# A GFNet and MLP layer on one core: the first stage done one tile at a time

## The chip, the core and the metric

The kernel runs on one NeuronCore of a Trainium2 chip. Five engines work side by side, each through its own instructions in order: TensorE (PE in the profile, with its weight loads shown as PEld), VectorE (DVE), ScalarE (ACT), GpSimd (POOL) and SyncE (SP), which here only issues transfers between HBM and the on-chip memory SBUF. The engines wait for each other on semaphores. The metric is the device time of one execution, in microseconds; lower is better.

## The reference

One batch of S = 2048 rows with D = 576 channels goes through a spectral filter and then an MLP with 4608 hidden channels, each behind a layer norm, each with a residual. Everything is fp32.

```python
def _layernorm(x, axis=-1, eps=1e-5):
    m = jnp.mean(x, axis=axis, keepdims=True)
    v = jnp.var(x, axis=axis, keepdims=True)
    return (x - m) / jnp.sqrt(v + eps)
...
        X = jnp.fft.rfft2(x, axes=(-2, -1))      # x: layer norm of A_x
        X = X * (w_r + 1j * w_i)
        y = jnp.fft.irfft2(X, s=(S, D), axes=(-2, -1))
...
        h = jnp.einsum("bsd,df->bsf", x, w1)     # x: layer norm of h
        h = jnp.maximum(h, zero)
        return jnp.einsum("bsf,fd->bsd", h, w2)
...
    h = x + _A_ref(_layernorm(x, axis=-1), A_w_r, A_w_i)
    h2 = h + _B_ref(_layernorm(h, axis=-1), B_w1, B_w2)
```

## The kernel before

The transforms are matrix products with constant cosine and sine tables. The program has four stages, one behind the other on TensorE.

The first stage takes the 16 tiles of x (128 rows by 576 channels each; rows 16 apart lie in one tile) through the layer norm and the first step of the transform over the rows. The normalisation is folded into other work. VectorE takes mean and variance of a tile (two `bn_stats` of 288 channels, `stat1`, then one `bn_aggr`), turns them into variance plus epsilon and minus twice the mean (two small operations, `scal1`), and GpSimd raises the first to the power -0.5 (`pow1`). The real transform over 576 channels needs only sums and differences of channel n and channel 576 - n. GpSimd writes the differences of a tile into every second column of a buffer G (`sub1`), VectorE writes the sums, less twice the mean, into the other columns (`add1`, line 262) and column 0 with an operation of its own (line 263). That is called the fold here. ScalarE scales a 128x192 cosine table with the tile's inverse deviation (`cs1`, line 269), so that TensorE multiplies G by a table that already holds the normalisation (`fwd_a`, the products of line 155), and ScalarE copies the product out of PSUM into `zx` (line 158). The last tile does its short products first and has part of its output copied by VectorE.

Before this stage TensorE runs 36 transposes of the identity (`warm_pe(WARM)`, line 300), which compute nothing that is used.

The order of the first stage is written out by hand in the loop at line 303. The 16 tiles form 11 parts: tiles 0 to 3 alone, tiles 4 to 13 in pairs, tiles 14 and 15 alone. For a part the code issues the difference, the statistics, the small operations and the power; then the products of the part before, with the table scaling of this part put ahead of the last of them; then the sums of this part. No scheduler moves anything (`manual_schedule`): each engine does its share in just this order. Buffers are the ring `e` of ten (`ebuf`), of which a part takes two, one for G and one for its tables; a constant for the second stage holds a further one throughout.

The second stage (`mid_l`, `mid_d`, `mid_b`, `mid_i`) does the transform over the channels, the rest of that over the rows, the filter and the first step back, in 16 steps p, with four blocks of tables and filter weights (FB into C, W into B, IB into D). The third undoes the transform, adds x, which is loaded a second time into the memory that `zx` held (line 460), and prepares the second layer norm. The fourth is the MLP.

All loads of the first two stages are issued on SP's queue in one fixed order, except two on ScalarE's: x by tile (tiles 4 to 15 in pairs, each pair as two transfers of 64 rows), the constants for the second stage (line 181), then the four blocks. Transfers take eight semaphores in turn, so an issue waits until the transfer eight issues earlier has landed. None of these issues waits for an engine until line 320, behind the last block.

Of the kernel before, what the change touches and what calls it, by code (L numbers as in the profile page):

```python
# [12 lines left out]
AF = mybir.ActivationFunctionType  # L13
ALU = mybir.AluOpType
PSUM = bass.MemoryType.PSUM

S, D, DFF = 2048, 576, 4608
NK = D // 2 + 1
NT = 16
NP = 16  # L20
EPS = 1e-5
# [1 line left out]
NG = DFF // (128 * GF)  # L23
CH = 4
NC = NT // CH
WARM = 36
EB = 10
EW = 1344
GW = D + 2
# [93 lines left out]
def dims(ap, off, *pairs):  # L123

    return bass.AP(tensor=ap.tensor, offset=ap.offset + off, ap=[list(ap.ap[0]), *[list(p) for p in pairs]])
# [3 lines left out]
def kernel(ctx: ExitStack, tc: tile.TileContext, x, w_r, w_i, w1, w2, cc2, c1, fb, ib, c3, out):  # L129
    nc = tc.nc  # L130
# [5 lines left out]
    def sb(shape, tag, bufs=1, dt=F32):  # L136
        n[0] += 1
        return pool.tile(shape, dt, tag=tag, name=f"{tag}_{n[0]}", bufs=bufs)
# [3 lines left out]
    def ps():  # L142
        n[0] += 1
        if banks:
            return banks[0].tile([128, 1024], F32, tag="w", name=f"w_{n[0]}", bufs=2)
        return psum.tile([128, 1024], F32, tag="d", name=f"d_{n[0]}", bufs=4)
# [3 lines left out]
    def ebuf(shape, dt=F32):  # L150
        e = sb([128, EW], "e", EB, dt)[:, :int(np.prod(shape[1:]))]
        return e.rearrange("p (a b) -> p a b", a=shape[1]) if len(shape) == 3 else e

    def mm(o, l, r, start, stop):
        nc.tensor.matmul(o, l, r, start=start, stop=stop)  # L155

    def act(o, i, **kw):
        nc.scalar.activation(o, i, AF.Copy, **kw)  # L158

    xs = sb([128, NT, D], "X")  # L160
# [14 lines left out]
    caf, cai = ccs[:, :192], ccs[:, 192:]  # L175
# [30 lines left out]
    half = sb([128, 2], "half")  # L206
# [19 lines left out]
    lfv = cst[:, 580:].rearrange("p (a n) -> p a n", a=2)  # L226
    Fs = {}

    stats = {}
    parts = [(t, 1) for t in range(4)] + [(t, 2) for t in range(4, NT - 2, 2)] + [(NT - 2, 1), (NT - 1, 1)]  # L230
    mvs, Gs = {}, {}

    def stat1(g):
        t0, k = parts[g]
        st, mv, r = sb([128, k, 2, 6], "st", 2), sb([128, k, 2], "mv", 3), sb([128, 3, k], "r", 3)
        for i in range(k):
            for h in range(2):
                nc.vector.bn_stats(st[:, i, h, :], xs[:, t0 + i, 288 * h:288 * h + 288])  # L238
            nc.vector.bn_aggr(mv[:, i, :], st[:, i].rearrange("p a b -> p (a b)"))  # L239
        mvs[g] = mv, r  # L240

    def scal1(g):
        mv, r = mvs[g]
        nc.vector.tensor_scalar(r[:, 0, :], mv[:, :, 1], EPS, None, op0=ALU.add)
        nc.vector.tensor_scalar(r[:, 2, :], mv[:, :, 0], -2.0, None, op0=ALU.mult)

    def pow1(g):
        r = mvs[g][1]
        nc.gpsimd.tensor_tensor(r[:, 1, :], r[:, 0, :], half[:, :parts[g][1]], op=ALU.pow)

    def sub1(g):
        t0, k = parts[g]
        G = Gs[g] = ebuf([128, 2, GW])
        a, b = dims(xs, t0 * D + 1, [D, k], [287, 2], [1, 144]), dims(xs, t0 * D + 575, [D, k], [-287, 2], [-1, 144])
        nc.gpsimd.tensor_sub(dims(G, 575, [GW, k], [1, 2], [-2, 144]), a, b)

    def add1(g):
        t0, k = parts[g]
        for i in range(k):
            o = (t0 + i) * D  # L260
            a, b = dims(xs, o + 1, [287, 2], [1, 144]), dims(xs, o + 575, [-287, 2], [-1, 144])
            nc.vector.scalar_tensor_tensor(dims(Gs[g], i * GW + 2, [-1, 2], [2, 144]), a, mvs[g][1][:, 2, i:i + 1], b, op0=ALU.add, op1=ALU.add)  # L262
            nc.vector.tensor_scalar(Gs[g][:, i, 0:1], xs[:, t0 + i, 0:1], 2.0, mvs[g][1][:, 2, i:i + 1], op0=ALU.mult, op1=ALU.add)

    def cs1(g):
        t0, k = parts[g]
        c, r = ebuf([128, 2, 192]), mvs[g][1]
        for i in range(k):
            nc.scalar.activation(c[:, i, :], caf, AF.Copy, scale=r[:, 1, i:i + 1])
            Fs[t0 + i] = Gs[g][:, i, :], c[:, i, :]  # L270

    def fwd_a(t):
        G, caf = Fs.pop(t)
        p = ps()

        def rest(p):
            for e in range(2):
                for j in range(2):
                    q = slice(64 * j, 64 * j + 64)
                    mm(p[64 * e:64 * e + 64, 512 * j + 256:512 * j + 320], G[q, 256:320], caf[q, :64], True, True)  # L280

        end = t == NT - 1
        if end:
            p2 = ps()
            rest(p2)
            nc.vector.tensor_copy(dims(zx, 8192 + 2 * t, [32, 64], [1, 2]), dims(p2, 256, [1, 64], [512, 2]))
        for h in range(2):
            for k in range(2):
                for j in range(2):
                    q = slice(64 * j, 64 * j + 64)  # L290
                    mm(p[:, 512 * j + 128 * h:512 * j + 128 * h + 128], dims(G[q], (k, 321 - k)[h], [2, 128]),
                       caf[q, 64 * k:64 * k + 128], k == 0, k == 1)
        if not end:
            rest(p)
        act(dims(zx, 2 * t, [2048, 5 - end], [32, 64], [1, 2]), dims(p, 0, [64, 5 - end], [1, 64], [512, 2]))

    def warm_pe(k):
        wm = ps()
        for _ in range(k):
            nc.tensor.transpose(wm[:, :128], ident, ident)  # L300

    warm_pe(WARM)
    for g in range(len(parts) + 1):
        last = g == len(parts)
        if not last:
            sub1(g)
            stat1(g)
            scal1(g)
            pow1(g)
        old = [parts[g - 1][0] + i for i in range(parts[g - 1][1])] if g else []  # L310
        for t in old[:-1]:
            fwd_a(t)
        if not last:
            cs1(g)
        for t in old[-1:]:
            fwd_a(t)
        if not last:
            add1(g)
    c3t = ebuf([128, 1160])
    nc.sync.dma_start(c3t, c3)  # L320
    raw, wts = {}, {}
# [7 lines left out]
    def leftover():  # L329
        v4 = sb([128, 2, 256], "G")  # L330
        nc.gpsimd.memset(v4, 0.0)
        return v4
# [117 lines left out]
    xs = xa[:, :NT * D].rearrange("p (t d) -> p t d", t=NT)  # L450
# [711 lines left out]
```

## Time and profile before

Three runs of the kernel took 991.18, 991.42 and 992.99 us; the median is 991.42. The profile below is of one further execution.

| | |
|---|---|
| profiled execution, its own time | 992.26 us |
| its span, first to last instruction | 990.4 us |
| what lies around the span | 1.86 us |
| TensorE clock granted over the span | 0.998 |
| TensorE busy | 971.9 us (98%) |
| VectorE busy | 764.1 us (77%) |
| GpSimd busy | 586.2 us (59%) |
| ScalarE busy | 450.5 us (45%) |

Four stretches of the same execution, cut where TensorE begins and ends the second stage and where the third stage is under way:

| stretch, us | PE busy | DVE busy | ACT busy | POOL busy | clock granted |
|---|---|---|---|---|---|
| 0 to 36.6 | 30.14 | 29.64 | 17.73 | 20.40 | 0.95 |
| 36.6 to 92.4 | 55.80 | 43.33 | 23.62 | 0.00 | 1.00 |
| 92.4 to 118 | 23.53 | 22.42 | 10.29 | 9.55 | 1.00 |
| 118 to 990.4 | 862.41 | 668.68 | 398.86 | 556.21 | 1.00 |

In a row of the timeline the first number is the start in microseconds from the span's beginning, the second the duration, then come the engine, the line of the kernel, the operation, the tiles it writes and reads, the shape and a count; in square brackets stands how long the engine had been idle and what released it. "SPq" and "DVEq" are an engine's queue of issues and waits. An operation may start while the one ahead of it on its engine still drains, so the step from start to start is what a row costs the engine, and it is often shorter than the duration. The chain of work that ended last is read as start, length and what it was.

### The profile page before, as it was taken

The numbers are of one execution on the slowest core, as the hardware profiler recorded it, in microseconds if no ns is written. First come the engines' busy times: TensorE is split into PE (matmuls) and PEld (weight loads), VectorE is DVE, ScalarE is ACT, GpSimd is POOL, SyncE is SP. The second block draws the span as 40 slices with busy tenths as digits, with TensorE's granted clock in tenths as the row PEclk, the third lists the DMA queues.
The fourth block names the chain that finished last, engine by engine and source line by source line (L and its number), as shares of the span: only waits on it lengthen the run. The fifth ranks groups of instructions, "written<-read, shape, count | busy, mean of one in ns | idle before, by whom it ended". The sixth has DMA issues, their size and how long they took to land.

```text
span 990.4 us, 18038 instructions
## 1 busy us (share of the span) xinstructions
PE 971.9 (98%) x6708; PEld 861.6 (87%) x6708; DVE 764.1 (77%) x1206; ACT 450.5 (45%) x870; POOL 586.2 (59%) x714
## 2 busy tenths in 40 slices
PE   7999999999999999999999999999999999999997
PEld 7777668999998899999999999999999999999997
DVE  7788877437654888888888888878888888878886
ACT  4445355513323545445444554544454544544541
POOL 5201365502235768687677777687767777686741
PEclk9999999999999999999999999999999999999999
DMA  9953623457598471818365472818274453809365
GB/s 233 231 148 105 143 94 126 161 163 249 179 323 275 177 260 59 300 49 289 96 224 165 154 241 80 294 41 303 76 245 145 174 195 125 288 32 319 103 211 144
DMA packets 122727, 178.71 MB, mean 180 GB/s; under 512 B 7568, under 2 KB 102288, under 8 KB 122640
## 3 DMA queue, kind: packets, MB, share of 16 engines
q1 hardware_dynamic: 121904, 176.67, 55.5%
q8 instruction: 53, 0.87, 0.4%
q10 hardware_dynamic: 736, 0.89, 0.3%
q14 instruction: 34, 0.28, 0.1%
HBM read 153.15 MB, written 23.07 MB: 178 GB/s over the span
## 4 chain that ended last, share of the span: by engine, by line
PE 88%; DVE 5%; DMA 3%; issue 1%; ACT 1%; POOL 1%; SPq 0%; DVEq 0%; POOLq 0%; ACTq 0%
PE h L795 33%; PE w L900 33%; PE d L155 20%; DMA A<-in_A_x_dram 2%; DVE st L238 1%; DMA t1T<-e 1%; PE d L547 1%; PE w L155 1%; DVE e L262 0%; DVE A L910 0%; DVE A L505 0%; DMA X<-in_A_x_dram 0%; DVE mv L239 0%; ACT D L610 0%; PE h L900 0%
## 5 line engine op out<-in xcount | busy, mean ns | idle before, releaser
L910 DVE TENSOR_TENSOR A<-A,w 128x576 f32<-128x576 f32 x415 | 307.1, 751 | 83.9 <-PE w L900 71.2
L900 PE MATMUL w<-X,D 128*128 128x288 f32 x1416 | 217.3, 295 | 0.4 <-ACT e L614 0.3
L900 PEld LDWEIGHTS w<-X,D 128*128 128x128 f32 x1416 | 204.4, 188 | 10.5 <-ACT e L614 0.5
L795 PE MATMUL h<-B,e 128*128 128x512 f32 x630 | 160.7, 394 | 1.5 <-DVE A L604 0.9
L158 ACT ACTIVATE e<-h 128x512 f32<-128x512 f32 x90 | 53.9, 598 | 183.5 <-PE h L795 183.5
L795 PEld LDWEIGHTS h<-B,e 128*128 128x128 f32 x630 | 113.2, 188 | 22.0 <-issue 1.1
L345 POOL TENSOR_TENSOR e<-e,e 128x512 fp32r<-128x512 f32 (+3 forms) x61 | 78.4, 1285 | 57.9 <-ACT e L158 52.7
L795 PE MATMUL h<-X,e 128*128 128x512 f32 x420 | 106.1, 392 | 0.0
L614 ACT ACTIVATE e<-e 128x512 f32<-128x512 f32 x90 | 57.0, 633 | 105.8 <-DVE e L853 46.6
L345 POOL TENSOR_TENSOR X<-e,X 128x576 fp32r<-128x576 f32 (+1 forms) x32 | 46.9, 1468 | 73.9 <-ACT X L158 73.9
L795 PEld LDWEIGHTS h<-X,e 128*128 128x128 f32 x420 | 75.7, 188 | 12.8
L158 ACT ACTIVATE e<-e 128x256 fp32r<-128x256 f32 (+5 forms) x162 | 74.5, 489 | 26.5 <-DMA t1T<-e 13.2
L819 POOL TENSOR_TENSOR A<-e 128x256 f32<-128x256 f32 x59 | 46.4, 786 | 27.1 <-DVE X L809 27.1
L809 DVE TENSOR_TENSOR D<-A,D 128x512 fp32r<-128x512 f32 x59 | 60.9, 1032 | 0.9 <-ACT D L158 0.9
L900 PEld LDWEIGHTS w<-X 128*128 128x128 f32 x360 | 53.8, 188 | 5.6 <-issue 0.7
L900 PE MATMUL w<-X 128*128 128x288 f32 x360 | 57.1, 294 | 0.5 <-DVE A L910 0.5
L900 PE MATMUL w<-X,e 128*128 128x288 f32 x348 | 55.5, 295 | 0.0
L155 PE MATMUL d<-e,D 128*128 128x288 f32 x384 | 53.4, 296 | 0.0
L155 PEld LDWEIGHTS d<-e,D 128*128 128x128 f32 x384 | 52.4, 188 | 1.1 <-issue 0.2
L795 PE MATMUL h<-C,e 128*128 128x512 f32 x210 | 53.3, 393 | 0.0
L795 PE MATMUL h<-F,e 128*128 128x512 f32 x210 | 53.2, 392 | 0.0
L821 POOL TENSOR_TENSOR A<-e,A 128x256 f32<-128x256 f32 x59 | 51.2, 867 | 0.8 <-DVE A L817 0.8
(168 smaller groups left out, 1857.6 us busy)
## 6 DMA issues: line engine op xcount, KB each, us to landing
X<-t0T SPq DMA_DIRECT2D x16, 768.0 KB, 8.1
X<-t1T SPq DMA_DIRECT2D x16, 768.0 KB, 7.6
e<-in_B_w_dram SPq DMA_DIRECT2D x18, 576.0 KB, 3.8
e<-in_B_w_dram SPq DMA_DIRECT2D x18, 512.0 KB, 3.8
X<-t0T SPq DMA_DIRECT2D x16, 512.0 KB, 8.7
X<-t1T SPq DMA_DIRECT2D x16, 512.0 KB
B<-t0T SPq DMA_DIRECT2D x8, 768.0 KB
F<-t0T SPq DMA_DIRECT2D x8, 768.0 KB
```

The lines of the kernel that those rows point to most:

```text
L155: nc.tensor.matmul(o, l, r, start=start, stop=stop)
L158: nc.scalar.activation(o, i, AF.Copy, **kw)
L238: nc.vector.bn_stats(st[:, i, h, :], xs[:, t0 + i, 288 * h:288 * h + 288])
L345: eng.tensor_sub(l, v, h)
L547: nc.tensor.transpose(pz[:, 128 * ORDER[b]:128 * ORDER[b] + 128], y[:, 128 * b:128 * b + 128], ident)
L614: nc.scalar.activation(o, i, AF.Relu)
L795: nc.tensor.matmul(o, a, b, start=bool(first) and n_ == 0, stop=n_ == len(ops) - 1, skip_group_check=not first)
L809: (eng or nc.vector).tensor_sub(f[1], v, f[0])
L819: nc.gpsimd.tensor_sub(s3, p0[:, :256], p0[:, 256:])
L821: nc.gpsimd.tensor_sub(s4, p1_[:, :256], s2)
L900: nc.tensor.matmul(P[tt], l[:, q], r, start=first and n_ == 0, stop=end and n_ == 2, skip_group_check=whole and not first)
L910: nc.vector.tensor_add(xt, xt, P)
```

## The change

The parts are gone; the stage goes through single tiles. In step t of the loop VectorE does the first half of tile t's statistics, the two small operations of tile t-1, the second half of tile t's statistics, the sums of tile t-1, and the aggregation of tile t. GpSimd does the power of tile t-1 and then the differences of tile t. ScalarE scales the table of tile t-1 and now writes column 0 of G for it too, in place of VectorE. The products are those of tile t-2, where they were those of the part before. G and the scaled table of a tile share one buffer of the ring. There are 30 warm-up transposes in place of 36.

```diff
-WARM = 36
+WARM = 30
...
+    def first(t):
+        if t not in firsts:
+            e = ebuf([128, GW + 192])
+            firsts[t] = e[:, :GW], e[:, GW:], sb([128, 2, 6], "st1", 3), sb([128, 2], "mv1", 3), sb([128, 3], "r1", 4)
+        return firsts[t]
...
+    def row1(t):
+        mv, r = first(t)[3:]
+        nc.vector.tensor_scalar(r[:, 0:1], mv[:, 1:2], EPS, None, op0=ALU.add)
+        nc.vector.tensor_scalar(r[:, 2:3], mv[:, 0:1], -2.0, None, op0=ALU.mult)
...
     def add1(g):
-        for i in range(k):
-            nc.vector.scalar_tensor_tensor(dims(Gs[g], i * GW + 2, [-1, 2], [2, 144]), a, mvs[g][1][:, 2, i:i + 1], b, op0=ALU.add, op1=ALU.add)
-            nc.vector.tensor_scalar(Gs[g][:, i, 0:1], xs[:, t0 + i, 0:1], 2.0, mvs[g][1][:, 2, i:i + 1], op0=ALU.mult, op1=ALU.add)
+        nc.vector.scalar_tensor_tensor(dims(G, 2, [-1, 2], [2, 144]), a, r[:, 2:3], b, op0=ALU.add, op1=ALU.add)
...
+    def scale1(t):
+        G, c, _, _, r = first(t)
+        nc.scalar.activation(c, caf, AF.Copy, scale=r[:, 1:2])
+        nc.scalar.activation(G[:, 0:1], xs[:, t, 0:1], AF.Identity, bias=r[:, 2:3], scale=2.0)
+        Fs[t] = firsts.pop(t)[:2]
...
     warm_pe(WARM)
-    for g in range(len(parts) + 1):
-        last = g == len(parts)
-        if not last:
-            sub1(g)
-            stat1(g)
-            scal1(g)
-            pow1(g)
-        old = [parts[g - 1][0] + i for i in range(parts[g - 1][1])] if g else []
-        for t in old[:-1]:
-            fwd_a(t)
-        if not last:
-            cs1(g)
-        for t in old[-1:]:
-            fwd_a(t)
-        if not last:
-            add1(g)
+    sub1(0)
+    for t in range(NT + 2):
+        if t < NT:
+            stat1(t, 0)
+        if 1 <= t <= NT:
+            row1(t - 1)
+            pow1(t - 1)
+        if t < NT:
+            stat1(t, 1)
+        if 1 <= t <= NT:
+            add1(t - 1)
+        if 1 <= t < NT:
+            sub1(t)
+        if t < NT:
+            aggr1(t)
+        if 1 <= t <= NT:
+            scale1(t - 1)
+        if t >= 2:
+            fwd_a(t - 2)
```

What stands on VectorE for the pair of tiles 6 and 7 before (`X` is x, `st` and `mv` the statistics, `r` the small operations' results, `e` the buffer G):

```order
L238 BN_STATS st_324<-X_63 128x6 x2
L239 BN_AGGR mv_325<-st_324 128x2
L238 BN_STATS st_324<-X_63 128x6 x2
L239 BN_AGGR mv_325<-st_324 128x2
L244 TENSOR_SCALAR r_326<-mv_325 128x2
L245 TENSOR_SCALAR r_326<-mv_325 128x2
L262 SCALAR_TENSOR_TENSOR e_322<-X_63,r_326 128x2x144
L263 TENSOR_SCALAR e_322<-X_63,r_326 128x1
L262 SCALAR_TENSOR_TENSOR e_322<-X_63,r_326 128x2x144
L263 TENSOR_SCALAR e_322<-X_63,r_326 128x1
```

On VectorE in the changed kernel, for tiles 5 and 6:

```order
L242 BN_STATS st_39_286<-X_63 128x6
L250 TENSOR_SCALAR r_36_260<-mv_35_259 128x1
L251 TENSOR_SCALAR r_36_260<-mv_35_259 128x1
L242 BN_STATS st_39_286<-X_63 128x6
L263 SCALAR_TENSOR_TENSOR e_257<-X_63,r_36_260 128x2x144
L246 BN_AGGR mv_40_287<-st_39_286 128x2
L242 BN_STATS st_44_314<-X_63 128x6
L250 TENSOR_SCALAR r_41_288<-mv_40_287 128x1
L251 TENSOR_SCALAR r_41_288<-mv_40_287 128x1
L242 BN_STATS st_44_314<-X_63 128x6
L263 SCALAR_TENSOR_TENSOR e_285<-X_63,r_41_288 128x2x144
L246 BN_AGGR mv_45_315<-st_44_314 128x2
```

Between an operation and the one that needs its result there now stands a half of another tile's statistics; column 0 (line 263 before) is gone from this engine.

GpSimd for the same tiles before, where `half` holds the exponent:

```order
L255 TENSOR_TENSOR e_287<-X_63 128x2x2x144
L249 TENSOR_TENSOR r_291<-r_291,half_143 128x2
L255 TENSOR_TENSOR e_322<-X_63 128x2x2x144
L249 TENSOR_TENSOR r_326<-r_326,half_143 128x2
L255 TENSOR_TENSOR e_371<-X_63 128x2x2x144
```

and in the changed kernel:

```order
L255 TENSOR_TENSOR r_31_232<-r_31_232,half_143 128x1
L258 TENSOR_TENSOR e_257<-X_63 128x2x144
L255 TENSOR_TENSOR r_36_260<-r_36_260,half_143 128x1
L258 TENSOR_TENSOR e_285<-X_63 128x2x144
L255 TENSOR_TENSOR r_41_288<-r_41_288,half_143 128x1
L258 TENSOR_TENSOR e_313<-X_63 128x2x144
```

The differences come in single tiles (128x288) and each power stands right ahead of the differences of the next tile.

ScalarE in the changed kernel, where `cc` holds the table, `A` is `zx` and `d` a PSUM bank; before, the three rows per tile were two, without that of line 268:

```order
L267 ACTIVATE e_257<-cc_75,r_36_260 128x192
L268 ACTIVATE e_257<-X_63,r_36_260 128x1
L158 ACTIVATE A_147<-d_299 128x320x2
L267 ACTIVATE e_285<-cc_75,r_41_288 128x192
L268 ACTIVATE e_285<-X_63,r_41_288 128x1
L158 ACTIVATE A_147<-d_327 128x320x2
```

The copy out of PSUM that stands behind a tile's scaling is that of the tile before it. Behind the first stage the instructions of every engine stand as before; TensorE's products of the first stage are the same in number and order, and SP's issues are unchanged.

More of the change, by code (lines that the diff above doesn't have):

```diff
@@ L227 @@
     Fs = {}
[L229 to L235, printed above, removed]
-        for i in range(k):
[L237 to L270, printed above, removed]
+    stats, firsts = {}, {}
@@ new lines, in first, with pair, stat1, aggr1 @@
+    def first(t):
[3 more added lines that the diff above has]
+        return firsts[t]
+    def pair(t):
+        o = t * D
+        return dims(xs, o + 1, [287, 2], [1, 144]), dims(xs, o + 575, [-287, 2], [-1, 144])
+    def stat1(t, h):
+        nc.vector.bn_stats(first(t)[2][:, h, :], xs[:, t, 288 * h:288 * h + 288])
+    def aggr1(t):
+        _, _, st, mv, _ = first(t)
+        nc.vector.bn_aggr(mv, st.rearrange("p a b -> p (a b)"))
@@ new lines, in row1, with pow1, sub1, add1 @@
+    def row1(t):
+        mv, r = first(t)[3:]
+        nc.vector.tensor_scalar(r[:, 0:1], mv[:, 1:2], EPS, None, op0=ALU.add)
+        nc.vector.tensor_scalar(r[:, 2:3], mv[:, 0:1], -2.0, None, op0=ALU.mult)
+    def pow1(t):
+        r = first(t)[4]
+        nc.gpsimd.tensor_tensor(r[:, 1:2], r[:, 0:1], half[:, :1], op=ALU.pow)
+    def sub1(t):
+        nc.gpsimd.tensor_sub(dims(first(t)[0], 575, [1, 2], [-2, 144]), *pair(t))
+    def add1(t):
+        G, _, _, _, r = first(t)
+        a, b = pair(t)
+        nc.vector.scalar_tensor_tensor(dims(G, 2, [-1, 2], [2, 144]), a, r[:, 2:3], b, op0=ALU.add, op1=ALU.add)
```

## The prediction

> **What bounds the kernel now.** I read the chain of waits first, then the first 40 us by stretches, then single rows. The chain, in order of time (start, length, what it was):
>
> ```profile
> 4.27 0.83 DVE st L238 x2
> ...
> 36.09 0.46 ACT e L269
> 36.59 55.82 PE d L155 x832
> 92.44 0.66 SPq L460
> ...
> 94.87 5.19 DMA A<-in_A_x_dram
> ...
> 110.50 1.40 DVE A L505 x2
> ```
>
> From 4.27 to 36.59 the chain is VectorE's, tile after tile. At 36.59 TensorE begins the last tile's products, and from there it is TensorE without a break to 92.4; the second load of x starts only when that is done. So whatever brings 36.59 forward brings the rest forward, as long as nothing behind it has an earlier hour of its own. The stretches, with busy time of PE, PEld, DVE, ACT, POOL, then granted clock, DMA share and GB/s:
>
> ```profile
> 0.00:10.00 10.00, 8.64 (x64) 8.29 (x66) 5.47 (x23) 2.52 (x5) 4.77 (x13) 1.00 0.77 206
> 10.00:20.00 10.00, 8.01 (x136) 6.93 (x134) 9.33 (x31) 6.40 (x12) 7.09 (x7) 1.00 1.03 236
> 20.00:30.00 10.00, 7.68 (x110) 6.34 (x107) 9.41 (x31) 4.32 (x8) 4.43 (x4) 0.83 1.00 245
> ```
>
> VectorE is 93 to 94% busy from 10 to 30, and the transfers run at full share. TensorE has gaps and once a lower clock. Here is what it does:
>
> ```profile
> 1.36 7.04 PE L300 MATMUL d<-ident 128*128 128x128 f32 x36 [1.36 <-POOL ident masks.py:199]
> 8.33 5.74 PE L155 MATMUL d<-e,e 64*128 64x128 f32 x96
> 23.73 4.32 PE L155 MATMUL d<-e,e 64*128 64x128 f32 x48 [1.83 <-ACT e L269]
> ```
>
> A tile is 24 products, so 5.74/4 = 1.435 us at full clock. Behind the gap of 1.83 us two tiles took 4.32 instead of 2.87.
>
> **VectorE's step per tile.** The prices are steps from start to start in these rows:
>
> ```profile
> 5.13 0.21 DVE L239 BATCH_NORM_AGGREGATE mv<-st 128x2 f32<-128x12 f32 x1
> 5.37 0.15 DVE L244 TENSOR_SCALAR r<-mv 128x1 f32<-128x1 f32 x1
> 5.44 0.14 DVE L245 TENSOR_SCALAR r<-mv 128x1 f32<-128x1 f32 x1
> 5.60 0.56 POOL L249 TENSOR_TENSOR r<-r,half 128x1 f32<-128x1 f32 x1 [0.48 <-DVE r L245]
> 5.62 0.52 DVE L262 SCALAR_TENSOR_TENSOR e<-X,r 128x288 f32<-128x288 f32 x1
> 6.05 0.21 DVE L263 TENSOR_SCALAR e<-X,r 128x1 f32<-128x1 f32 x1
> 6.14 0.81 POOL L255 TENSOR_TENSOR e<-X 128x288 f32<-128x288 f32 x1
> 6.18 0.45 DVE L238 BATCH_NORM_STATS2 st<-X 128x6 f32<-128x288 f32 x1
> 6.54 0.44 DVE L238 BATCH_NORM_STATS2 st<-X 128x6 f32<-128x288 f32 x1
> 12.79 0.21 DVE L239 BATCH_NORM_AGGREGATE mv<-st 128x2 f32<-128x12 f32 x1
> 12.91 0.77 DVE L238 BATCH_NORM_STATS2 st<-X 128x6 f32<-128x288 f32 x2
> 13.71 0.21 DVE L239 BATCH_NORM_AGGREGATE mv<-st 128x2 f32<-128x12 f32 x1
> 14.03 0.17 DVE L244 TENSOR_SCALAR r<-mv 128x2 f32<-128x2 f32 x1
> ```
>
> One half of the statistics steps 0.36 (6.18 to 6.54), a small operation 0.07 (5.37 to 5.44), the sums 0.43 (5.62 to 6.05), an aggregation with nothing waiting on it 0.12 (12.79 to 12.91). The new step is two halves, two small operations, sums and aggregation: 0.36 + 0.07 + 0.07 + 0.36 + 0.43 + 0.12 = 1.41. What goes is column 0 (0.13, 6.05 to 6.18) and the waits of an operation for the one right ahead of it, since each now has a half of another tile's statistics in between. Before, a tile took 1.91 alone (4.27 to 6.18).
>
> What the trace does not show is whether the extra semaphores cost. The small operation now waits, from tile 4 on, for two engines beside its own, the sums from tile 9 on for one. Behind an aggregation the small operation came 0.24 later in the first tile and 0.32 later at 13.71, where it had one more semaphore to wait for: 0.08 each. Hidden under the 0.44 us of statistics ahead of them they cost nothing, unhidden 0.24 for three. That gives 1.41 to 1.65. I take 1.50, one of the three unhidden: what stands ahead is now longer than the 0.21 of an aggregation, so most should hide.
>
> **x has to be there.** Since a transfer is issued only when the one eight before has landed, the last two issues for x tell when tiles 6 and 7 landed:
>
> ```profile
> SPq L166 <- DMA X<-in_A_x_dram: 1.2, 2, 0.8
> 12.10 0.47 SPq L166 DMA_DIRECT2D X<-in_A_x_dram  x1
> 13.35 0.47 SPq L166 DMA_DIRECT2D X<-in_A_x_dram  x1
> ```
>
> They waited 1.2 us in all, so the halves of 6 and 7 landed about 12.1 and 13.35, 1.25 apart, and tiles 4 and 5 at about 10.9 (an estimate, two halves ahead). VectorE would reach tile 4 at 4.27 + 0.98 + 3 x 1.5 = 9.75 (0.98 is tile 0: its aggregation starts 0.86 in and steps 0.12), so it waits there for 1.1 us. From then on x comes at 1.25 us per tile, faster than 1.50, and no longer binds: tile 6 is wanted at 13.9.
>
> **Sum.** Tile 4 starts at 10.9. Twelve steps of 1.50 bring the end of the last aggregation's step to 28.9, its start to 28.8. From the start of the last aggregation to the last tile's products the path (small operations, power, scaling) is unchanged; before it took:
>
> ```profile
> 34.88 0.21 DVE L239 BATCH_NORM_AGGREGATE mv<-st 128x2 f32<-128x12 f32 x1
> 36.09 0.46 ACT L269 ACTIVATE e<-cc,r 128x192 f32<-128x192 f32 x1 [0.26 <-POOL r L249]
> ```
>
> 36.59 - 34.88 = 1.71. So the last products start at 30.5, which is 6.1 us earlier. With 1.65 per tile it is 32.3 (4.3 earlier), with 1.41 29.4, but TensorE cannot follow: tile 3's products wait for tile 4's first statistics, 10.9 + 0.36, then 1.40 from the small operation to products (1.71 less the 0.31 between aggregation and small operation), then about 0.15 for column 0: 12.8, and twelve tiles of 1.435 end the wait at 30.0 (6.6 earlier). Gain 4.3 to 6.6, likeliest 6.1.
>
> **The other parts.** Warm-up: six transposes fewer at 7.04/36 each end it 1.2 us earlier, about 7.2, when tile 0's operands arrive. Even from 8.33 three tiles of 1.435 would be through at 12.6, ahead of tile 3's 12.8: worth nothing, hidden by the wait for x. If that wait were shorter it would be worth up to 1.1. Clock: no gap over 0.7 us is left by these numbers, so I expect 1.00 through 20 to 30. Column 0 on ScalarE:
>
> ```profile
> 3.32 0.20 ACT L209 ACTIVATE warm<-half 128x1 f32<-128x1 f32 x1
> 9.88 0.76 ACT L158 ACTIVATE A<-d 128x640 f32<-128x640 f32 x1 [1.32 <-PE d L155]
> 10.52 0.44 ACT L269 ACTIVATE e<-cc,r 128x192 f32<-128x192 f32 x1
> ```
>
> ScalarE per tile: copy 0.64 (9.88 to 10.52), scaling 0.44, column 0 0.20, together 1.28 and under 1.50. Behind the copy stands the next scaling, and TensorE waits for that two tiles on: about 0.1 + 1.28 from the end of a tile's products, against the 1.435 of the tile in between. It fits by 0.05; unhidden it costs about half its excess per tile, 0.6 in all if ScalarE takes 0.1 more. GpSimd per tile: power 0.54 (5.60 to 6.14) and differences 0.80, 1.34, plus what it waits for VectorE, below.
>
> **Later stages.** The second stage's first filter product on VectorE, with TensorE's product ahead of it:
>
> ```profile
> 41.23 1.20 PE L155 MATMUL d<-e,C 128*64 128x289 f32 x8
> 42.53 0.76 DVE L406 TENSOR_TENSOR e<-d,B 128x578 f32<-128x578 f32 x1 [5.23 <-DMA B<-in_A_w_i_dram]
> ```
>
> It would move to 36.4. It needs x, constants and the first block's FB and W, 7.2 MB in queue order; by the stretches 2.06 + 2.36 + 2.45 = 6.9 MB are in at 30, so it is there at about 32 (an estimate). TensorE's end at 42.43 released it, in my reading.
>
> The sum against the execution's own time: 992.26 - 6.1 = 986.2. That execution lies 0.84 above the median of the runs; against the median, 991.42 - 6.1 = 985.3.
>
> **Rivals.** *The port (slower).* VectorE's sums and GpSimd's differences get in each other's way:
>
> ```profile
> 14.28 0.70 POOL L249 TENSOR_TENSOR r<-r,half 128x2 f32<-128x2 f32 x1 [0.98 <-DVE r L245]
> 14.86 0.51 DVE L262 SCALAR_TENSOR_TENSOR e<-X,r 128x288 f32<-128x288 f32 x1
> 14.94 1.71 POOL L255 TENSOR_TENSOR e<-X 128x576 f32<-128x576 f32 x1
> 18.40 1.73 DVE L262 SCALAR_TENSOR_TENSOR e<-X,r 128x288 f32<-128x288 f32 x1
> 18.41 1.41 POOL L255 TENSOR_TENSOR e<-X 128x576 f32<-128x576 f32 x1
> ```
>
> Ahead by 0.08 the sums take 0.51 and the differences 1.71, 0.30 more; side by side (0.01) the sums take 1.2 more. In the new order, counted from the second small operation, the sums start at 0.07 + 0.36 = 0.43 and the differences at 0.16 + 0.54 = 0.70 (5.44 to 5.60, then the power): the sums lead by 0.27 and win. GpSimd's worst is 1.34 + 0.30 = 1.64 per tile, inside the range. If instead the power, which starts at 0.16, held the sums off until the differences took over, they would start at 1.50, 1.07 late: a step of 2.5. Then tile 4 starts at 5.25 + 3 x 2.5 = 12.8, the last products at 12.8 + 30 + 1.6 = 44.4 (1.6 is 1.71 less the aggregation's 0.12), 7.8 later than now: 999. It turns slower once 5.25 + 15 steps + 1.6 passes 36.59, at a step of 1.98, so when the sums lose 0.5 per tile. Against it: at 14.86 the sums start inside a power's 14.28 to 14.98 and still take their 0.51.
>
> [...]
>
> *Absorbed (no change).* If the row at 42.53 means what it says, and a late transfer released the filter product, the second stage cannot start earlier and the gain is lost: 991.4. For it the 5.23 us put down to DMA, against it the bytes above.
>
> *Less.* ScalarE's round trip, GpSimd's 1.64 and a low clock together make a step of 1.65 to 1.80: the last products at 10.9 + 12 x 1.8 + 1.6 = 34.1, gain 2.5 to 4.3: 987.1 to 988.9. For it: four engines between 1.28 and 1.50 leave little play.
>
> **How the numbers follow.** Forecast (984.8 to 987.1) 0.72, less gain 0.12, absorbed 0.08, port 0.08. The three runs spread over 1.8 us, 0.2%, about what can be told from no change. Faster by more than 2 us: forecast and "less", 0.84; same 0.08; slower 0.08. The range goes from 984.3, the lower bound with half a microsecond of that spread, to 988.8, through nearly all of "less": it leaves out the two other cases and a few hundredths, 0.8 held.
>
> **What would show it.** Right: halves of the statistics of successive tiles 1.4 to 1.6 apart behind tile 4, a wait for x ahead of tile 4, sums of 0.51 throughout, clock 1.00 in 20 to 30, the last tile's products at 30 to 32, the second load of x issued about 86. Wrong: sums of 1.2 us or more; VectorE idle until 42 in front of the filter product; a second stage longer than 55.8 us.

## The result and the profile after

The changed kernel took 987.46 us (median of five runs, 986.55 to 988.77) against 991.40 for the kernel before on the same chip (five runs, 991.18 to 992.99). The ratio is 0.9959, with a 95% interval of 0.9944 to 0.9973: a gain of 3.9 us, with 2.7 to 5.6 in the interval. Forecast were 985.3 and a gain of 6.1, in a range of 984.3 to 988.8.

Between the two profiled executions the gain is larger: 992.26 - 987.46 = 4.80 us. The traces are compared on that footing. The profiled execution before lay 0.84 above the median of its kernel, the one after is the median itself, and 4.80 - 0.84 is the 3.9 of the medians.

The chain of work that ended last, of the kernel after, in order of time (start, length, what it was):

```profile
5.98 5.51 DMA X<-in_A_x_dram
...
11.59 0.46 DVE st L242
...
13.46 7.22 PE d L155 x117
20.68 1.01 issue
21.68 66.01 PE d L155 x1003
87.71 0.66 SPq L463
...
105.78 1.41 DVE A L508 x2
```

Before, this chain was VectorE's, tile after tile, until 36.59. Now it is a transfer of x until 11.5, two microseconds that the chain puts down to VectorE, and from 13.46 TensorE, but for a stop of 1.01 us at 20.68 that the chain calls "issue": the engine waited for nothing that the profile shows. In the two microseconds the program's order tells more than the chain: behind VectorE's small operations of tile 3 (12.02) stand GpSimd's power (12.18), ScalarE's scaling (12.77) and column 0, the last that tile 3's products read:

```profile
13.13 0.28 ACT L268 ACTIVATE e<-X,r 128x1 f32<-128x1 f32 x1
```

It ends at 13.41, right ahead of the products at 13.46; the small operation (line 250) that the profile names as their releaser is tile 4's, which they do not read. The second load of x is issued at 87.71 where it was 92.44, its end is at 105.78 where it was 110.50: 4.73 and 4.72 of the 4.80 us are already there, so the whole gain is made in the first stage and carried to the end.

The stretches after (PE, PEld, DVE, ACT, POOL, clock, DMA share, GB/s):

```profile
10.00:20.00 10.00, 8.77 (x150) 7.50 (x148) 8.66 (x39) 7.75 (x19) 8.61 (x13) 1.00 1.03 235
20.00:30.00 10.00, 8.99 (x150) 7.66 (x148) 8.72 (x39) 7.64 (x20) 9.43 (x15) 1.00 1.02 253
```

From 20 to 30 the clock is 1.00 where it was 0.83, TensorE has 150 products in ten microseconds where it had 110 to 136, and four engines stand between 7.6 and 9.4 us busy of 10. TensorE's timeline of the first stage:

```profile
7.56 1.49 PE L155 MATMUL d<-e 64*128 64x128 f32 x24 [0.38 <-ACT e L268]
9.32 2.90 PE L155 MATMUL d<-e 64*128 64x128 f32 x48 [0.28 <-DVE r L250]
13.46 7.22 PE L155 MATMUL d<-e 64*128 64x128 f32 x117 [1.23 <-DVE r L250]
21.68 11.60 PE L155 MATMUL d<-e 64*64 64x64 f32 x195 [1.01 <-issue]
33.21 3.34 PE L155 MATMUL d<-e,A 64*64 64x290 f32 x48
```

From tile 3 on TensorE waits for no other engine. The second stage begins at 33.21, with the row that reads `e,A`. The same row of the kernel before:

```profile
38.01 3.34 PE L155 MATMUL d<-e,A 64*64 64x290 f32 x48
```

So the second stage begins 4.80 earlier. One step of the new order, with statistics of tiles 7 and 8 and sums of tiles 6 and 7:

```profile
16.11 0.45 DVE L242 BATCH_NORM_STATS2 st<-X 128x6 f32<-128x288 f32 x1
16.25 0.55 POOL L255 TENSOR_TENSOR r<-r,half 128x1 f32<-128x1 f32 x1
16.48 0.50 DVE L263 SCALAR_TENSOR_TENSOR e<-X,r 128x288 f32<-128x288 f32 x1
16.77 0.87 POOL L258 TENSOR_TENSOR e<-X 128x288 f32<-128x288 f32 x1
...
17.02 0.40 DVE L242 BATCH_NORM_STATS2 st<-X 128x6 f32<-128x288 f32 x1
17.34 0.13 DVE L250 TENSOR_SCALAR r<-mv 128x1 f32<-128x1 f32 x1
17.39 0.14 DVE L251 TENSOR_SCALAR r<-mv 128x1 f32<-128x1 f32 x1
17.45 0.45 DVE L242 BATCH_NORM_STATS2 st<-X 128x6 f32<-128x288 f32 x1
17.82 0.50 DVE L263 SCALAR_TENSOR_TENSOR e<-X,r 128x288 f32<-128x288 f32 x1
```

From the second half of one tile's statistics to that of the next (16.11 to 17.45), and from sums to sums (16.48 to 17.82), it is 1.34 us. The sums take 0.50, and the differences, which begin 0.29 behind them, 0.87. Last, the second stage's first filter product:

```profile
37.67 0.76 DVE L409 TENSOR_TENSOR e<-d,B 128x578 f32<-128x578 f32 x1 [5.17 <-DMA B<-in_A_w_r_dram]
```

It was at 42.53 and moved by 4.86, with the same wait put down to the same kind of transfer.

### The profile page after: what moved, and what is told of

It is laid out like the page before. It is cut to its first block, busy times and chain, and to the rows that moved or that the text cites. A ratio compares the mean times of both kernels' runs of the same rounds, so it can differ in the third digit from the quotient of the medians.

```text
span 985.6 us, 18055 instructions
## 1 busy us (share of the span) xinstructions
PE 970.0 (98%) x6702; PEld 859.7 (87%) x6702; DVE 756.8 (77%) x1200; ACT 453.5 (46%) x886; POOL 588.4 (60%) x724
## 4 chain that ended last, share of the span: by engine, by line
PE 92%; DVE 3%; DMA 2%; ACT 1%; SPq 1%; issue 1%; DVEq 0%
PE h L798 34%; PE w L903 33%; PE d L155 24%; DMA A<-in_A_x_dram 2%; PE d L550 1%; PE w L155 1%; DMA X<-in_A_x_dram 1%; DVE A L913 0%; SPq L166 0%; DVE A L508 0%; PE h L903 0%; DVE st L215 0%; DVE D L614 0%; ACT D L613 0%; SPq L463 0%
## 5 line engine op out<-in xcount | busy, mean ns | idle before, releaser
L798 PEld LDWEIGHTS h<-X,e 128*128 128x128 f32 x420 | 75.7, 188 | 12.8
```

The costliest lines, as they stand in the source:

```text
L798: nc.tensor.matmul(o, a, b, start=bool(first) and n_ == 0, stop=n_ == len(ops) - 1, skip_group_check=not first)
```

## The experiments

Each kernel is timed against the kernel before on its own chip. Moments of a trace are given for the start of the second stage (33.21 after, 38.01 before) and for the issue of the second load of x (87.71 and 92.44).

**The interleaving undone, all else kept.** The edit of the kernel after:

```diff
     sub1(0)
-    for t in range(NT + 2):
+    for t in range(NT + 1):
         if t < NT:
             stat1(t, 0)
-        if 1 <= t <= NT:
-            row1(t - 1)
-            pow1(t - 1)
-        if t < NT:
             stat1(t, 1)
...
             aggr1(t)
...
+            row1(t)
+            pow1(t)
+            add1(t)
+            if t + 1 < NT:
+                sub1(t + 1)
+            scale1(t)
+        if t >= 1:
+            fwd_a(t - 1)
```

> The changed kernel with a tile's work in the old order: both halves of the statistics, aggregation, small operations, power, sums, then the next tile; single tiles, column 0 on ScalarE, the shared buffer and 30 transposes stay. Theory (the interleaving is nearly the whole gain): VectorE's step is the 2.04 of the kernel with all tiles alone less 0.13 for column 0, 1.91; fifteen steps from 4.4, then 0.86 and 1.71, put the last products at 35.6 and the second stage at 37.0, 1.0 ahead of the kernel before: 990.7. Rival (the gain comes from column 0, the buffers and the single tiles): 988 or less, second stage at 34 or earlier.

Measured: 990.73 us (990.53 to 991.27) against 992.20, ratio 0.9981 (0.9972 to 0.9990). The second stage begins at 36.43. VectorE's timeline of this kernel, a tile's statistics each:

```profile
15.20 0.81 DVE L242 BATCH_NORM_STATS2 st<-X 128x6 f32<-128x288 f32 x2
17.08 0.81 DVE L242 BATCH_NORM_STATS2 st<-X 128x6 f32<-128x288 f32 x2
```

The step is 1.88 us (1.95 in the later tiles), with no column 0 on VectorE and with single tiles. The interleaving alone takes it to 1.34; of the 4.80 us at the start of the second stage, 36.43 - 33.21 = 3.2 are the interleaving's, with the stop of 1.01 in the kernel after and none in this one. The other 1.6 belong to everything else in the change.

**Single tiles alone.** The edit of the kernel before:

```diff
-    parts = [(t, 1) for t in range(4)] + [(t, 2) for t in range(4, NT - 2, 2)] + [(NT - 2, 1), (NT - 1, 1)]
+    parts = [(t, 1) for t in range(NT)]
```

> The kernel before with all 16 tiles alone, nothing else. Theory (three of the pairs lost 1.2 us each at the port, and the order costs 1.91 per tile): fifteen steps of 1.91 from 4.3, then 0.86 and 1.71, put the last products at 35.5, 1.1 earlier than the kernel before: 990.3. No sums over 0.6. Rival (pairs cost nothing, only the interleaving gains): 991.4, last products at 36.6. Rival (single tiles are nearly all of the gain): 988 or less.

Measured: 991.61 us (991.31 to 993.03) against 991.78, ratio 0.9994 (0.9985 to 1.0003). TensorE's timeline of this kernel, two successive tiles:

```profile
28.86 1.49 PE L155 MATMUL d<-e,e 64*128 64x128 f32 x24 [0.55 <-ACT e L269]
30.89 1.49 PE L155 MATMUL d<-e,e 64*128 64x128 f32 x24 [0.55 <-ACT e L269]
```

The tiles come 2.03 us apart, not at the 1.91 of the first tile from which 990.3 was worked out. The pairs before had the same pace: from tile 4's aggregation to tile 15's it was (34.88 - 12.79)/11 = 2.01 per tile. So smaller parts by themselves bring nothing that can be told from no change, though all sixteen sums take 0.52 here and two of the kernel before took 1.7: what the pairs lost there, single tiles lose in waits. The extra 0.12 per tile is unhidden. The small operation comes 0.31 behind the aggregation where it was 0.25 in the first tiles, and the sums come 0.25 behind the second small operation where it was 0.18; in front of each stands only something short.

**Column 0 back on VectorE.** The edit of the kernel after:

```diff
         nc.vector.scalar_tensor_tensor(dims(G, 2, [-1, 2], [2, 144]), a, r[:, 2:3], b, op0=ALU.add, op1=ALU.add)
+        nc.vector.tensor_scalar(G[:, 0:1], xs[:, t, 0:1], 2.0, r[:, 2:3], op0=ALU.mult, op1=ALU.add)
...
-        nc.scalar.activation(G[:, 0:1], xs[:, t, 0:1], AF.Identity, bias=r[:, 2:3], scale=2.0)
```

> The changed kernel with column 0 written by VectorE again, behind the sums. Theory (TensorE sets the pace at 1.435 us per tile, VectorE has play): VectorE's step goes from 1.34 to 1.47, twelve of them from 11.6 end at 29.2, and the last tile's products could start at 30.7, ahead of the 31.7 where TensorE gets to them: no change, 987.5 within 0.8. Rival (VectorE sets the pace): 12 x 0.13 = 1.6 later, 989. Rival (column 0 on ScalarE holds TensorE up): up to 0.6 earlier.

Measured: 987.11 us (986.55 to 987.54), ratio 0.9948 (0.9936 to 0.9961), the kernel after within the uncertainty. TensorE's timeline of this kernel:

```profile
13.18 7.33 PE L155 MATMUL d<-e 64*128 64x128 f32 x117 [0.98 <-ACT e L268]
21.29 11.52 PE L155 MATMUL d<-e 64*64 64x64 f32 x195 [0.78 <-issue]
```

Tile 3's products, the stop (0.78) and the pace behind it are nearly those of the kernel after. VectorE's step is now 1.47 (aggregations at 12.89 and 14.36), a little over TensorE's 1.435. Over twelve tiles that is 0.4 us, less than TensorE loses at its stop, so it need not show. The move of column 0 brings nothing that can be told here; without the stop it might.

**36 warm-up transposes again.** The edit of the kernel after:

```diff
-WARM = 30
+WARM = 36
```

> The changed kernel with 36 warm-up transposes. Theory (tile 3's products wait for x, not for the warm-up): no change against the changed kernel, 987.5 within 0.8; the second stage still begins at 33.2 and the second load of x is still issued at 87.7, each within 0.5. Rival (the shorter warm-up is part of the gain): both about 1.0 later. The gap of 1.0 us on TensorE inside tile 7's products (20.68 to 21.68, put down to issue): if it belongs to a place in TensorE's stream of instructions, it moves about half a tile of products earlier, since six transposes are added ahead of it; if it belongs to a time, it stays at 20.7; if it belongs to the products, it stays three products before the end of tile 7.

Measured: 988.82 us (986.27 to 989.58), ratio 0.9958 (0.9944 to 0.9972); the profiled execution took 989.58, the second stage began at 34.57, the second load of x at 89.06. TensorE's timeline of this kernel:

```profile
13.02 6.97 PE L155 MATMUL d<-e 64*128 64x128 f32 x111 [0.84 <-DVE r L250]
21.45 13.19 PE L155 MATMUL d<-e 64*128 64x128 f32 x201 [1.46 <-issue]
```

and its stretches:

```profile
20.00:22.00 2.00, 0.56 (x11) 0.29 (x10) 2.00 (x9) 0.14 (x1) 2.00 (x4) 1.00 1.02 237
22.00:24.00 2.00, 2.00 (x26) 1.66 (x28) 1.68 (x8) 1.38 (x4) 1.63 (x3) 0.67 1.02 276
24.00:26.00 2.00, 2.00 (x24) 1.78 (x24) 2.00 (x11) 1.13 (x3) 2.00 (x4) 0.50 1.04 355
```

Time and moments missed the expectation: the time by 1.3 us, the second stage and the second load by 1.4, about where the rival put them. The rows say that it was not the warm-up. Tile 3 starts no later than with 30 transposes (13.02 against 13.46). The stop is 0.45 longer than after, and behind it TensorE takes 13.12 us to the second stage where it took 11.53; six products more explain 0.36 of this, the lower clock about 1.2. The times of this kernel, 986.27 to 989.58, spread too far to tell a microsecond. And the stop is at another product: 111 of them after tile 3's start where it was 117. With 36 + 72 + 111 = 219 transposes and products ahead of it here and 30 + 24 + 48 + 117 = 219 after, the stop is tied to a place in TensorE's stream of instructions, not to a tile. VectorE and GpSimd were busy all through it (2.00 of 2.00). Behind it the clock fell to 0.67 and 0.50 here; behind the 1.01 of the kernel after it stayed 1.00.

**The kernel after, once more.** No edit.

> The changed kernel once more, unchanged, beside the others. Theory (its times spread because the block of TensorE's instructions lands at another time in each execution): the gap after 219 products is there again with another length, 0.5 to 1.5 us, and the times spread over more than 1 us; 987.5. Rival (the gap was an accident of one execution): no gap, times within 0.5 of each other, 986.5.

Measured: 986.53 us (986.17 to 987.53), against 991.72 for the kernel before on that chip, ratio 0.9942 (0.9928 to 0.9955). The stop is there again, behind the same 30 + 24 + 48 + 117, and 1.20 us long:

```profile
21.82 11.60 PE L155 MATMUL d<-e 64*64 64x64 f32 x195 [1.20 <-issue]
```

So it belongs to the kernel, with a length that changes from run to run. By medians the gain is 5.2 us here, where the first set gave 3.9: its size is known to about a microsecond, and 986.53 is as far below the 987.5 that I expected. The times of the four sets of runs with the stop spread over 1.0 to 3.3 us, those of the next four kernels, whose profiles have none, over 0.5 to 1.2.

**What the stop may wait for.** The profile of the kernel after counts 53 packets, 0.87 MB in all and 16 KB each, on a queue that it calls "instruction". TensorE's 2 x 6702 products and weight loads make 253 for each packet, so I take the packets for blocks of TensorE's instructions and the one below for the first of them. That is an estimate from this count and the queue's name; the profile does not name the engine. The queue over the whole span, and in a narrow window with its first packet (packets, MB, share):

```profile
q8 instruction: 53, 0.87, 0.4%
q8 instruction: 1, 0.02, 39.6%
```

The second row is that of 18.9 to 19.1 us. The products resumed 2.7 us after the packet's start at 19.03; with 36 transposes the packet started at 18.5 and the products resumed 3.0 later, with column 0 on VectorE at 18.7 and 2.6 later, in the repetition at 18.9 and 2.9 later.

The twelve profiles of this case agree with this. In the four with the stop the packet had started only 1.2 to 1.6 us ahead of the 219th transpose or product. In the eight without it, TensorE came to the 220th 2.7 us (the sums behind the differences, below) to 6.3 us (all tiles one by one, below) behind the packet's start and ran on. In none of the twelve did the 220th start less than 2.6 us behind the packet.

The 16 DMA engines were then at full share (1.08 from 18 to 20 in the kernel after) with transfers of x in pairs of tiles. Three kernels test whether the block waits behind these: x of some tiles is loaded tile by tile, in transfers of 144 KB in place of 288.

Tiles 4 to 7 one by one:

```diff
-    for i in range(2, 8):
+    for t in range(4, 8):
+        load_x(xs, t, 1)
+    for i in range(4, 8):
         load_x(xs, 2 * i, 2)
```

> The changed kernel with tiles 4 to 7 loaded one by one in place of in pairs. Theory (the first stage waits for the pair 4 and 5 at 11.6, and TensorE follows from there at its own pace): tile 4 lands about 1.2 earlier, tile 3's products start at 12.3 in place of 13.5, and the last products, the second stage and the second load of x all come 1.0 to 1.2 earlier: 986.4. Rival (VectorE or TensorE binds elsewhere): no change, 987.5. Rival (four more issues of 0.64 delay the later tiles of x): up to 1 later.

Measured: 986.25 us (985.68 to 986.88), ratio 0.9941 (0.9928 to 0.9953). The second stage begins at 31.27. TensorE's timeline of this kernel:

```profile
7.67 10.28 PE L155 MATMUL d<-e 64*128 64x128 f32 x168 [1.40 <-ACT e L270]
18.23 3.02 PE L155 MATMUL d<-e 64*128 64x128 f32 x48 [0.28 <-ACT e L270]
21.43 9.91 PE L155 MATMUL d<-e 64*128 64x128 f32 x168 [0.19 <-ACT e L270]
```

The wait for x ahead of tile 4 is gone, and so is the stop; the block came at 14.6. Both changed at once, which the next two take apart.

Tiles 4 and 5 alone:

```diff
-    for i in range(2, 8):
+    load_x(xs, 4, 1)
+    load_x(xs, 5, 1)
+    for i in range(3, 8):
         load_x(xs, 2 * i, 2)
```

> The changed kernel with only tiles 4 and 5 loaded one by one. It separates the two things that loading 4 to 7 one by one did. Theory A (tile 4's landing and TensorE's gap are separate; the gap is a block of TensorE's instructions that waits behind the transfers in flight, which are as long here as in the changed kernel): tile 3's products at 12.2 in place of 13.5, the gap of about 1.0 after 219 products stays, second stage at 32.0. Rival B (the gap hangs on when TensorE gets there, not on the transfers in flight): no gap, second stage at 31.1.

Measured: 986.52 us (986.18 to 986.63), ratio 0.9939 (0.9926 to 0.9953), the second stage at 32.33. TensorE's timeline of this kernel:

```profile
16.05 2.91 PE L155 MATMUL d<-e 64*128 64x128 f32 x48 [0.69 <-DVE r L252]
19.27 1.49 PE L155 MATMUL d<-e 64*128 64x128 f32 x24 [0.32 <-DVE mv L248]
20.97 11.43 PE L155 MATMUL d<-e 64*128 64x128 f32 x192 [0.21 <-ACT e L270]
```

The stop that I expected did not come. The block was there at 17.3, with pairs still in flight, 3.2 us ahead of the product at which TensorE had stopped. VectorE waited for x at tile 6 in place of tile 4 (0.99 us, at 14.18), and TensorE's first gap follows from this. Its second, ahead of tile 7, follows from the sums of tile 7:

```profile
18.00 1.13 DVE L265 SCALAR_TENSOR_TENSOR e<-X,r 128x288 f32<-128x288 f32 x1
18.02 0.79 POOL L260 TENSOR_TENSOR e<-X 128x288 f32<-128x288 f32 x1
```

The sums led the differences by only 0.02 here and took 1.13 in place of 0.50. So this kernel tells little about the stop, but it shows that an earlier tile 4 alone moves the wait for x on to the next pair, and that a lead of 0.02 was not enough for the sums.

Tiles 8 to 15 one by one, 4 to 7 in pairs as after:

```diff
-    for i in range(2, 8):
+    for i in range(2, 4):
         load_x(xs, 2 * i, 2)
+    for t in range(8, NT):
+        load_x(xs, t, 1)
```

> The changed kernel with tiles 8 to 15 loaded one by one, 4 to 7 in pairs. Theory A (the block of instructions waits behind the transfers in flight, which are half as long here): tile 3's products at 13.4 as in the changed kernel, no gap after 219 products, second stage at 32.2, and the block's own transfer some microseconds ahead of the 19.0 that it had. Rival B: the gap stays and the second stage begins at 33.2.

Measured: 986.42 us (986.21 to 987.07), ratio 0.9940 (0.9928 to 0.9953). TensorE's timeline of this kernel:

```profile
13.23 18.51 PE L155 MATMUL d<-e 64*128 64x128 f32 x312 [1.03 <-DVE r L252]
31.66 3.34 PE L155 MATMUL d<-e,A 64*64 64x290 f32 x48
```

Tile 3 waits for tile 4's x as after (13.23 and 13.46), but from there 312 products run without a stop, and the block came at 14.6. Only transfers of x that are in flight around the block's packet were made smaller here, no instruction of TensorE's products was touched, and the stop is gone. That fits my reading of a block that waits behind transfers already in flight; no row shows such a wait. It is not the whole account: with all pairs in flight the block came at 16.7 in the kernel before, at 15.9 with single tiles alone and at 17.3 with the interleaving undone. The time cannot be told from that of the repetition (986.53, on another chip). The second stage begins 1.55 earlier than after, of which the stop is 1.01.

**All of tiles 4 to 15 one by one.**

```diff
-    for i in range(2, 8):
-        load_x(xs, 2 * i, 2)
+    for t in range(4, NT):
+        load_x(xs, t, 1)
```

> The changed kernel with tiles 4 to 15 all loaded one by one. Theory (both effects together: tile 4 lands earlier, and the block of instructions comes early): no gap after 219 products, TensorE at its pace of 1.435 from 7.7 on, second stage at 31.0 to 31.3, 986.0. Rival (24 issues at 0.64 make x the bound, 1.28 per tile, with waits for x at several tiles): second stage at 31.7 or later.

Measured: 985.78 us (985.41 to 985.87), ratio 0.9933 (0.9921 to 0.9946). It is the best version: on the same chip the kernel after took 986.53 (986.17 to 987.53), and no run of the one reaches into the other's. TensorE's timeline of this kernel, and further on its first wait in the second stage:

```profile
7.78 22.90 PE L155 MATMUL d<-e 64*128 64x128 f32 x384 [0.31 <-DVE r L250]
30.61 3.34 PE L155 MATMUL d<-e,A 64*64 64x290 f32 x48
...
39.22 0.78 PE L155 MATMUL d<-D,e 128*64 128x128 f32 x12 [0.15 <-DVE e L416]
```

All 384 products of the first stage run without a gap from 7.78 on; at this pace only an earlier first product could shorten the stage. The second stage begins 2.60 earlier than after, but the second load of x is issued at 85.82, only 1.89 earlier: from the one to the other it is 55.2 us where it was 54.5. The first filter product and TensorE's product ahead of it show why:

```profile
33.83 1.20 PE L155 MATMUL d<-e,C 128*64 128x289 f32 x8
35.92 0.76 DVE L409 TENSOR_TENSOR e<-d,B 128x578 f32<-128x578 f32 x1 [6.02 <-DMA D<-in_ib_dram]
```

TensorE's product ends at 35.03, and the filter product starts 0.89 later; in the kernel after the two were 0.04 apart (37.63 and 37.67). Now a transfer of the second stage's first block bounds the stage, and 0.7 us is lost there. By what the filter product reads it is most likely one of the filter's weights (B); the D that the profile names it does not read. This is the rival called "absorbed", at its true place.

**The sums behind the differences.** The edit of the kernel after issues the sums of tile t-2 behind the first half of tile t's statistics, and keeps a tile's buffers on record until then:

```diff
-        Fs[t] = firsts.pop(t)[:2]
+        Fs[t] = first(t)[:2]
...
             stat1(t, 0)
+        if t >= 2:
+            add1(t - 2)
         if 1 <= t <= NT:
...
-        if 1 <= t <= NT:
-            add1(t - 1)
```

> The changed kernel with the sums of a tile issued a half of the statistics later, ahead of the small operations of the next tile; everything else in place. [...] Rival (sums and differences do not exclude each other here, the lead of 0.27 was not needed): step 1.34, TensorE sets the pace and the products come some 0.7 later than in the changed kernel: 988.

Measured: 990.72 us (990.29 to 991.84) against 992.20, ratio 0.9984 (0.9975 to 0.9992); the second stage at 36.61. The timeline of this kernel, one step:

```profile
15.11 0.80 POOL L258 TENSOR_TENSOR e<-X 128x288 f32<-128x288 f32 x1
15.43 0.79 DVE L263 SCALAR_TENSOR_TENSOR e<-X,r 128x288 f32<-128x288 f32 x1
...
16.87 0.80 POOL L258 TENSOR_TENSOR e<-X 128x288 f32<-128x288 f32 x1
17.19 0.80 DVE L263 SCALAR_TENSOR_TENSOR e<-X,r 128x288 f32<-128x288 f32 x1
```

With GpSimd ahead the sums take 0.79 and the differences keep 0.80; the step is 1.76 (15.43 to 17.19), and 3.4 us of the gain at the start of the second stage are gone (36.61 - 33.21). Where no differences run beside them, at 12.17 and at 32.81, the sums of this kernel take 0.50 and 0.47. So the rival's step of 1.34 did not hold. The price of the meeting is real, but small beside the 1.2 that the sums lost in the forecast's row at 18.40: the sums start 0.32 into the differences and end 0.31 after them, which adds 0.29 to the sums and 0.42 to the step.

## Why the prediction was right, and where it was off

**Right: the place and the kind of the gain.** VectorE's chain is gone from the path, the second stage moves as a whole (from its start to the second load of x 54.43 before and 54.50 after), and the end follows. The filter product moved by 4.86 with the product of TensorE's ahead of it, so TensorE had released it; "absorbed" did not hold at this size of gain and begins only some two microseconds further, as the last version with x tile by tile shows. The clock stayed at 1.00. Column 0 brought nothing that could be told, and the shorter warm-up did not move tile 3. The sums lead by 0.29 (0.27 in the forecast) and keep their 0.50 (0.54 in the last of the sixteen tiles), so the rival that the prediction calls the port fell; when the lead is taken from them by force, the step goes to 1.76 and the gain is mostly lost.

That the two meet at a port, as the rival's name and the expectation of single tiles alone have it, no run shows. What the runs show is how much sums and differences hold each other up: sums that started 0.32 behind took 0.79 in place of 0.50, but ended 0.31 behind the differences, sooner than if they had waited for them whole; and sums that started first by 0.01 (the forecast's row at 18.40, 1.73) or 0.02 (tiles 4 and 5 one by one, 1.13), as the profile has the starts, were themselves the ones held up. The power of 128x1, on which the rival's step of 2.5 rested, did not hold them up: at 16.48 the sums start inside a power that runs from 16.25 to 16.80, and take 0.50.

**Mis-sized: VectorE's step.** I took 1.50 between bounds of 1.41 and 1.65; it is 1.34, also outside the 1.4 to 1.6 that I had named as the sign of being right. All the extra semaphores are hidden under the statistics ahead of them; the small operations step 0.05 and 0.06, and the first half of the statistics 0.32 where I had 0.36. Thereby TensorE's 1.435 per tile set the pace, which was the lower bound of the sum (last products at 30.0, gain 6.6) and not its likeliest value (30.5).

**Mis-sized: the landing of tile 4.** I put it at 10.9, "two halves ahead" of tile 7's at an even 1.25 us. VectorE got tile 4 at 11.59, and tile 3's products came at 13.46 where the sum had 12.8: 0.66 lost. In the profile before no wait showed it: there VectorE came to tile 4 only at 11.94.

**Missing: TensorE's stop.** No rival and no term held it. From tile 3's products twelve tiles of 1.435 end at 13.46 + 17.22 = 30.68, and the 1.01 of the stop makes 31.69 for the last products, 4.9 ahead of the 36.59 before; measured at the start of the second stage, 4.80. So of the bound's 6.6, 0.66 went to x and 1.01 to the stop, and about 0.1 is unaccounted for. The second load of x came at 87.71, not at the 86 that I had named as a sign of being right. Of the likeliest 6.1 the traces gave 4.80, and the medians 3.9.

Of the 53 packets of 16 KB on the queue called "instruction", one at most shows in the products of the kernel after: they have a single wait that is put down to "issue", the 1.01 us. In the four profiles with the stop it was 0.78, 1.01, 1.20 and 1.46 us long.

What is shown and what is argued: that the stop is at a fixed instruction (219 in four profiles, one with another number of transposes) and that it is gone with smaller transfers of x is shown; with x in pairs it is also absent where the first stage is slower (before, single tiles alone, interleaving undone, sums behind the differences). That it is the block that TensorE waited for, and that the packet is such a block, is argued from the moments of all twelve profiles and from the count of packets, since no row names the releaser. What sets the moment of the block stays open: with only tiles 4 and 5 split it came early too (17.3), as it did in the kernel before (16.7) with all pairs in flight.

**Luck in the range.** 987.46 lies outside the band of the forecast itself (984.8 to 987.1) and inside that of "less" (987.1 to 988.9). But nothing that "less" names took place: VectorE's step was shorter than forecast, the clock was 1.00, and no engine held TensorE up behind tile 3. The range held the time because it was wide enough for a stop that was in no rival, and because the 0.5 us that a step 0.16 too long had put into the sum (30.5 against 30.0) made up for part of the two losses.

## What to carry to other kernels

Where an engine's operations wait for each other in a short chain, put work of the next tile between them before shortening the operations: here that was 3.2 of 4.8 us, single tiles alone were worth nothing that could be told (991.61 against 991.78), and the extra waits cost nothing once a half of the statistics stood ahead of them (the small operations stepped 0.05 and 0.06). When a bound is taken away, work out the next one as a sum of its own, here TensorE's products from the moment its data land, and ask what each piece of that waits for, down to the size of the transfers. Of two engines that hold each other up, as VectorE's sums and GpSimd's differences do here, keep the bounding one ahead by a few tenths of a microsecond: 0.29 was enough, 0.02 was not.

## What the runs showed of the hardware that was not expected

In four of twelve profiles TensorE stopped for 0.8 to 1.5 us at one place of its instructions, behind 219 transposes and products, while transfers filled the 16 engines (shares of 0.98 to 1.06 from 20 to 22). With single tiles of x in flight in place of pairs (tiles 8 to 15, and all of 4 to 15) the packet that I take for TensorE's first block came at 14.6 and 12.8 us instead of 19.0, and the stop did not occur. The product behind that place never started less than 2.6 us behind the start of that packet, in twelve profiles.

The clock fell to 0.67 and 0.50 after a gap of 1.46 us (36 transposes) and stayed at 1.00 after one of 1.01 (the kernel after). The length of one gap does not tell these apart: it stayed at 1.00 after 1.20 (the repetition) and fell to 0.70 and 0.50 from 14 to 18 us in the kernel with the sums behind the differences, whose last gap of over half a microsecond before that was 1.18 (up to 12.82).

GpSimd's differences lost only 0.07 us (0.87 for 0.80) where they started 0.29 behind VectorE's sums, and VectorE's sums lost 0.29 (0.79 for 0.50) where they started 0.32 behind the differences. They lost 0.63 (1.13 for 0.50) where they started 0.02 ahead of them.
